# Random-feature attention into a token and channel mixer: q and k transposed by the DMA engines instead of TensorE

## The chip, the cores and the metric

The kernel runs on one core of one Trainium2 chip. The metric is device time in microseconds (us) of one execution. The core has five engines that each work through their own instruction list in order: TensorE (PE, with its weight loads listed as PEld), VectorE (DVE), ScalarE (ACT), GpSimd (POOL) and SyncE (SP). Sixteen DMA engines move data; a transfer is issued from an engine's list, here from POOL (the queue `software_dynamic`, which can change the type on the way), or from SP and ACT (`hardware_dynamic`).

## What is computed

Batch 8, 8 heads, 576 tokens, head width 64, 128 random features; the mixer has a token width of 256 and a channel width of 1536.

```
def phi(x):                       # for q and k, both scaled by 64 ** -0.25
    h = einsum('bhsd,md->bhsm', x, omega) - sum(x * x) / 2
    return exp(h - max(h)) / sqrt(m)
kv  = einsum('bhsm,bhsd->bhmd', k_p, v);   z = sum_s(k_p)
num = einsum('bhsm,bhmd->bhsd', q_p, kv);  den = einsum('bhsm,bhm->bhs', q_p, z)
x = heads side by side of num / (den + 1e-6)            # [8, 576, 512]
u  = x + (relu(x^T @ w_tok1) @ w_tok2)^T                # mixes tokens
out = u + relu(u @ w_ch1) @ w_ch2                       # mixes channels
```

## The kernel before

Everything is computed in fp16 with fp32 sums. Tokens 0 to 511 of a batch are its main part (four per partition), tokens 512 to 575 its tail. Heads are handled in pairs (`hp`, four pairs a batch).

*Loads.* POOL issues all loads and casts fp32 to fp16 on the way: `load_qk` (L76), `load_qk_tail` (L90, L91), `load_v` (L83), `load_v_tail` (L96), and the weights `load_wtok` (L143 to L149), `load_wc1` (L160), `load_wc2` (L163).

*Attention.* The projection needs q and k with the head width on the partitions. `t_main` (L180) transposes eight 128 x 128 blocks (two heads' tokens by two) on TensorE into a PSUM tile `t_ps`, and DVE copies it to `qT` or `kT` (L182); four calls serve a batch. `t_tail` does the same for the tails of q and k (L189, L193). `q_proj` (L247) and `k_proj` (L258) multiply with `bd`, omega twice on a diagonal, and ACT takes the exponential (L197) into `q_p` and `k_p`; `q_tail` (L203) and `k_tail` (L218, four matmuls a batch) do the tail. `k_max` finds each token's largest feature on DVE (L270, L274), its reciprocal (L278), and POOL scales v by it (L279, `v_sc`); `k_tail_max` does that for the tail (L226 to L234). `kv` sums over tokens on TensorE, one head at a time (L290, tail L297), ACT copies the result (L301, `kv_sb`), `num` multiplies by `q_p` (L311, L315), and DVE and ACT divide (L317, L318, L325) into `xm` and `xt`.

*Mixer.* `tok1` (L338, L341), `tok2` (L354), `tok2_tail` (L365), a transpose of u (`tokT`, L377, L378), `ch1` (L392, ReLU on ACT L399) and `ch2` (L404, sum on DVE L413), then the store of `o_sb` by SP (L415; tails L419, L420). `o_sb` has four buffers.

*Order.* No scheduler decides: `at(place, fn, ...)` notes each piece with a place, and the pieces are written out sorted by it, which fixes the order of every engine's list. One step of the place is one head pair; batch b's attention has steps 4b to 4b+4, its token mixing 4(b+1)+0.85 to 4(b+1)+3.85, its channel mixing 4(b+2) to 4(b+3). So the first `ch1` comes at step 8, attention ends near step 33, and the last channel pass, over all tails, fills steps 40 to 44. Batch b is loaded from place 4(b-2)+2.0 on.

Of the kernel before, what the change touches and what calls it, by code (L numbers as in the profile page):

```python
# [9 lines left out]
FP32 = mybir.dt.float32  # L10
# [7 lines left out]
def kernel(  # L18
# [17 lines left out]
    nc = tc.nc  # L36
# [20 lines left out]
    opool = ctx.enter_context(tc.tile_pool(name="outp", bufs=4))  # L57
    pspool = ctx.enter_context(tc.tile_pool(name="ps", bufs=1, space=bass.MemoryType.PSUM))
# [9 lines left out]
    nat = {}  # L68

    def load_qk(b, heads, which):  # L70
        h0, h1 = heads
        src = q if which == "q" else k
        key = (which, b)
        if key not in nat:
            nat[key] = ldpool.tile([P, H, NJ * D], FP16, name=f"{which}_nat", tag=f"{which}_nat")
        nc.gpsimd.dma_start(  # L76
            out=nat[key][:, h0:h1, :],
            in_=src[b, h0:h1, 0:SM, :].rearrange("h (p j) d -> p h (j d)", j=NJ),
        )

    def load_v(b):
        nat["v", b] = ldpool.tile([P, H, NJ * D], FP16, name="v_nat", tag="v_nat")
        nc.gpsimd.dma_start(  # L83
            out=nat["v", b], in_=v[b, :, 0:SM, :].rearrange("h (p j) d -> p h (j d)", j=NJ)
        )

    def load_qk_tail(b):
        t = ldpool.tile([P, H, D], FP16, name="qk_tail", tag="qk_tail")
        nat["qkt", b] = t
        nc.gpsimd.dma_start(out=t[0:ST], in_=q[b, :, SM:S, :].rearrange("h p d -> p h d"))  # L90
        nc.gpsimd.dma_start(out=t[ST:P], in_=k[b, :, SM:S, :].rearrange("h p d -> p h d"))  # L91

    def load_v_tail(b):
        t = ldpool.tile([P, H, D], FP16, name="v_tail", tag="v_tail")
        nat["vt", b] = t
        nc.gpsimd.dma_start(out=t[ST:P], in_=v[b, :, SM:S, :].rearrange("h p d -> p h d"))  # L96

    omega_nat = wpool.tile([P, 2 * D], FP16, name="omega_nat")
    nc.gpsimd.dma_start(out=omega_nat[:, 0:D], in_=omega)
    nc.gpsimd.dma_start(out=omega_nat[:, D : 2 * D], in_=omega)  # L100
    load_qk(0, (0, 2), "q")
    load_qk(0, (0, 2), "k")
    ident16 = wpool.tile([P, P], FP16, name="ident16")
    make_identity(nc, ident16)
    load_qk(0, (2, 4), "q")
    load_qk(0, (2, 4), "k")
    load_qk_tail(0)
    load_v(0)
    load_v_tail(0)
    load_qk(0, (4, 8), "q")  # L110
    load_qk(0, (4, 8), "k")
# [5 lines left out]
    nc.vector.memset(w1t, 0.0)  # L117
# [3 lines left out]
    nc.vector.memset(w2t, 0.0)  # L121
# [6 lines left out]
    vsc_t = [wpool.tile([P, H, 72], FP16, name=f"vsc_t{i}") for i in range(2)]  # L128
    for t in xt:
        nc.vector.memset(t, 0.0)  # L130
    for t in q_pt:
        nc.vector.memset(t[:, 0:ST], 0.0)
        nc.vector.memset(t[:, SM + ST : SM + 2 * ST], 0.0)
    for t in vsc_t:
        nc.vector.memset(t[0:ST], 0.0)
# [5 lines left out]

    def load_wtok():
        nc.gpsimd.dma_start(  # L143
            out=w1m.rearrange("p j t -> p (j t)"),
            in_=moe_w_tok1[0:SM, :].rearrange("(p j) t -> p (j t)", j=NJ),
        )
        nc.gpsimd.dma_start(out=w1t[0:ST, 0, :], in_=moe_w_tok1[SM:S, :])
        nc.gpsimd.dma_start(out=w1t[ST:P, 1, :], in_=moe_w_tok1[SM:S, :])
        nc.gpsimd.dma_start(out=w2raw, in_=moe_w_tok2.rearrange("(i p) s -> p i s", p=P))  # L149
# [9 lines left out]
    def load_wc1():  # L159
        nc.gpsimd.dma_start(out=wc1, in_=moe_w_ch1.rearrange("(i p) c -> p i c", p=P))  # L160

    def load_wc2():
        nc.gpsimd.dma_start(out=wc2, in_=moe_w_ch2.rearrange("(i p) d -> p i d", p=P))  # L163
# [7 lines left out]
    live = {}  # L171


    def t_main(b, half, which):

        src = nat[which, b]
        ps = att_ps([P, 8, P], FP16, "t_ps")
        for i in range(8):
            h, pr = half * 4 + i // 2, i % 2
            nc.tensor.transpose(ps[:, i, :], src[:, h, pr * P : (pr + 1) * P], ident16)  # L180
        sb = apool.tile([P, 8, P], FP16, name=f"{which}T", tag=f"{which}T")
        nc.vector.tensor_copy(out=sb, in_=ps)  # L182
        live[which + "T", b, half] = sb

    def t_tail(b):
        src = nat["qkt", b]
        ps = att_ps([P, NU, P], FP16, "tt_ps")
        for hp in range(NU):
            nc.tensor.transpose(  # L189
                ps[:, hp, :], src[:, 2 * hp : 2 * hp + 2, :].rearrange("p h d -> p (h d)"), ident16  # L190
            )
        sb = apool.tile([P, NU, P], FP16, name="tailT", tag="tailT")
        nc.vector.tensor_copy(out=sb, in_=ps)  # L193
        live["tailT", b] = sb
# [4 lines left out]
    def q_tail(b):  # L199
        sb = live["tailT", b]  # L200
        ps = att_ps([P, SM], FP32, "qt_ps")
        for w in range(2):
            nc.tensor.matmul(  # L203
                ps[:, w * 256 : (w + 1) * 256],
                bd[:, w * M : (w + 1) * M],
                sb[:, :, 0:ST],
                start=True,
                stop=True,
            )
        exp(q_pt[b % 2][:, ST : ST + SM], ps)  # L210

    def k_tail(b, g):
        sb = live["tailT", b]
        if g == 0:
            live["kpt", b] = apool.tile([P, H, M], FP16, name="k_pt", tag="k_pt")
        ps = att_ps([P, 4, M], FP32, "kt_ps")
        for i in range(2):
            nc.tensor.matmul(  # L218
                ps[:, 2 * i : 2 * i + 2, :], sb[:, 2 * g + i, :], bd, start=True, stop=True
            )  # L220
        exp(live["kpt", b][:, 4 * g : 4 * g + 4, :], ps)

    def k_tail_max(b):
        kp = live["kpt", b]
        tmp = apool.tile([P, H, M // 2], FP16, name="mxt", tag="mxt")
        nc.vector.tensor_tensor(  # L226
            out=tmp[ST:P], in0=kp[ST:P, :, 0 : M // 2], in1=kp[ST:P, :, M // 2 : M], op=ALU.max
        )
        mx = apool.tile([P, H], FP16, name="kmt", tag="kmt")
        nc.vector.reduce_max(out=mx[ST:P], in_=tmp[ST:P], axis=AX.X)  # L230
        vs = vsc_t[b % 2]
        with nc.allow_low_precision(reason="fp16 operand of the matmul"):
            nc.vector.reciprocal(out=vs[ST:P, :, D], in_=mx[ST:P])
        nc.gpsimd.tensor_tensor(  # L234
            out=vs[ST:P, :, 0:D],
            in0=nat["vt", b][ST:P],
            in1=vs[ST:P, :, D : D + 1].broadcast_to((ST, H, D)),
            op=ALU.mult,
        )

    def q_proj(b, hp, w):
        sb = live["qT", b, hp // 2]
        if w == 0:
            live["qp", b, hp] = apool.tile([P, 2, 4, P], FP16, name="q_p", tag="q_p", bufs=3)
        ps = att_ps([P, 4, P], FP32, "q_ps")
        i0 = (hp % 2) * 4
        nc.tensor.matmul(  # L247
            ps, bd[:, w * M : (w + 1) * M], sb[:, i0 : i0 + 4, :], start=True, stop=True
        )
        exp(live["qp", b, hp][:, w], ps)  # L250

    def k_proj(b, hp, i):
        sb = live["kT", b, hp // 2]
# [3 lines left out]
        for pr in range(2):  # L257
            nc.tensor.matmul(  # L258
                ps[:, 2 * pr : 2 * pr + 2, :],
                sb[:, (hp % 2) * 4 + 2 * i + pr, :],  # L260
                bd,
                start=True,
                stop=True,
            )
        exp(live["kp", b, hp][:, i], ps)

    def k_max(b, hp):
# [9 lines left out]
        with nc.allow_low_precision(reason="fp16 operand of the matmul"):  # L277
            nc.vector.reciprocal(out=vs[:, :, D], in_=mx)  # L278
        nc.gpsimd.tensor_tensor(  # L279
            out=vs[:, :, 0:D],  # L280
            in0=nat["v", b][:, 2 * hp : 2 * hp + 2, :].rearrange("p h (j d) -> p (h j) d", d=D),
# [4 lines left out]
    def kv(b, hp, i):  # L286
        h = 2 * hp + i
        ps = att_ps([P, D + 1], FP32, "kv_ps")
        for j in range(NJ):
            nc.tensor.matmul(  # L290
                ps,
                live["kp", b, hp][:, i, j, :],
                live["vsc", b, hp][:, i * 4 + j, 0 : D + 1],
                start=(j == 0),
                stop=False,
            )
        nc.tensor.matmul(  # L297
            ps, live["kpt", b][:, h, :], vsc_t[b % 2][:, h, 0 : D + 1], start=False, stop=True
        )
        sb = apool.tile([P, D + 1], FP16, name="kv_sb", tag="kv_sb", bufs=4)  # L300
        nc.scalar.copy(out=sb, in_=ps)  # L301
        live["kv", b, h] = sb

    def num(b, hp, i):
# [3 lines left out]
        sb = live["kv", b, h]  # L308
        ps = att_ps([P, NJ + 1, D + 1], FP32, "num_ps")
        for j in range(NJ):  # L310
            nc.tensor.matmul(  # L311
                ps[:, j, :], live["qp", b, hp][:, j % 2, 2 * i + j // 2, :], sb, start=True, stop=True
            )
        c0 = ST + (h % 2) * 256 + hp * ST - (b % 2) * ST
# [107 lines left out]

    def load_batch(b):
        load_qk(b, (0, H), "q")
        load_qk(b, (0, H), "k")
        load_qk_tail(b)
# [3 lines left out]
    at(0.02, load_wtok)  # L430
    at(0.30, load_batch, 1)
    at(0.60, load_wc1)
    at(0.90, load_wc2)
    at(1.2, permute_w2)
    for b in range(2, B):
# [78 lines left out]
```

The softmax here doesn't subtract the row's maximum and nothing guards it: scores larger than these inputs give would overflow.

## Time and profile before

| what | value |
|---|---|
| median of 3 runs | 348.16 us (347.2 to 349.61) |
| profiled execution, its own time | 348.58 us |
| its span, first to last instruction | 346.8 us |
| TensorE busy in the span | 310.2 us (89%) |
| DVE, ACT, POOL busy | 176.3, 173.5, 89.0 us |
| DMA issues from POOL, q and k of one batch | 512 KB each, 6.2 and 8.2 us to landing (medians) |
| stores from SP, 256 KB | 2.3 us to landing (median) |

The page cuts the span into 40 equal slices and gives each engine's busy share in tenths, the clock granted to TensorE in tenths, and the DMA engines' share and rate. Below it stand the chain of waits that ended last, groups of instructions by line, and DMA issues. A size in KB of a DMA issue is that of its fp16 destination where it casts. Matmuls are pipelined: the start of one to the start of the next tells what it costs, its own duration does not.

### The profile page before, as it was taken

The page shows a single profiled execution, that of the slowest core. Times are in us where ns is not written, and L with a number is a line of the kernel's source. Part 1 is how long each engine was busy: PE and PEld are TensorE (multiplying, and loading weights), DVE is VectorE, ACT ScalarE, POOL GpSimd, SP SyncE. Part 2 cuts the span into 40 slices and gives each one's busy share as a digit, 9 for nine tenths or more (in the row PEclk, how much of TensorE's full clock was granted, in tenths as well). Part 3 has the DMA queues.
Part 4 walks back from the last instruction along what each step waited for, and adds up shares of the span by engine and source line. Part 5 has one row for each costly group of instructions (what it writes and reads, how often), then busy time and mean ns, then how long its engine had stood idle before and what let it go on. Part 6 is the DMA issues. An engine that isn't in the chain of part 4 may idle for free.

```text
span 346.8 us, 5958 instructions
## 1 busy us (share of the span) xinstructions
PE 310.2 (89%) x2337; PEld 170.4 (49%) x2337; DVE 176.3 (51%) x423; ACT 173.5 (50%) x397; POOL 89.0 (26%) x106
## 2 busy tenths in 40 slices
PE   1537666999999999999999999999999899999994
PEld 1324344555655565556555655565555444444441
DVE  2546679546764575557654755576546414302011
ACT  1426663973397338743774378436753450160620
POOL 8687264243114411350225012011211100000000
PEclk9958999999999999999999999999999999999999
DMA  6999999309400950096009800011001001102013
GB/s 71 160 193 208 206 194 191 41 7 188 104 30 3 176 121 30 2 154 143 32 1 135 163 32 0 32 47 46 1 32 60 33 0 60 62 0 91 32 30 92
DMA packets 45916, 27.78 MB, mean 80 GB/s; under 512 B 14144, under 2 KB 40640, under 8 KB 45888
## 3 DMA queue, kind: packets, MB, share of 16 engines
q0 software_dynamic: 40640, 17.96, 41.3%
q1 hardware_dynamic: 5248, 9.44, 7.7%
q8 instruction: 18, 0.29, 0.3%
q14 instruction: 10, 0.08, 0.1%
HBM read 35.91 MB, written 9.44 MB: 131 GB/s over the span
## 4 chain that ended last, share of the span: by engine, by line
PE 77%; DVE 9%; ACT 4%; POOL 4%; DMA 3%; issue 2%; DVEq 0%; ACTq 0%; POOLq 0%
PE h_ps L392 27%; PE h_ps L404 25%; PE h_ps L338 3%; PE k_ps L258 3%; PE ht_ps L354 3%; PE q_ps L247 3%; PE t_ps L180 3%; DMA w1m<-in_moe_w_tok_dram 3%; PE num_ps L311 2%; DVE xm L318 2%; PE kv_ps L290 2%; DVE km L274 2%; ACT k_p L197 1%; ACT q_p L197 1%; PE uT_ps L377 1%
## 5 line engine op out<-in xcount | busy, mean ns | idle before, releaser
L404 PE MATMUL h_ps<-wc,r 128*128 128x512 f16 x432 | 98.1, 379 | 0.5 <-DVE ut L372 0.4
L392 PE MATMUL h_ps<-uT,wc 128*128 128x512 f16 x384 | 94.2, 379 | 3.7 <-DVE uT L378 3.7
L399 ACT ACTIVATE r<-h_ps 128x512 f16<-128x512 f32 x108 | 64.3, 601 | 46.2 <-PE h_ps L392 45.3
L279 POOL TENSOR_TENSOR v_sc<-v_nat,v_sc 128x512 f16<-128x512 f16 x32 | 34.1, 1065 | 164.5 <-DVE rc L317 81.5
L404 PEld LDWEIGHTS <-r 128*128 128x128 f16 x432 | 41.2, 98 | 46.2 <-issue 1.2
L392 PEld LDWEIGHTS <-wc 128*128 128x128 f16 x432 | 40.1, 98 | 42.6 <-issue 4.7
L325 ACT ACTIVATE xt<-num_ps,rc 64x64 f16<-64x64 f32 x64 | 19.7, 309 | 63.4 <-DVE xm L318 33.8
L197 ACT ACTIVATE k_p<-k_ps 128x512 f16<-128x512 f32 x64 | 37.7, 603 | 23.9 <-PE k_ps L258 23.9
L413 DVE TENSOR_TENSOR o_sb<-um,h_ps 128x512 f32<-128x512 f16 x32 | 21.9, 686 | 54.3 <-PE h_ps L404 54.3
L270 DVE TENSOR_TENSOR mx<-k_p 128x512 f16<-128x512 f16 x32 | 13.5, 422 | 51.9 <-ACT k_p L197 51.9
L197 ACT ACTIVATE q_p<-q_ps 128x512 f16<-128x512 f32 x64 | 36.4, 594 | 5.8 <-PE q_ps L247 5.2
L318 DVE TENSOR_TENSOR xm<-num_ps,rc 128x256 f16<-128x256 f32 x64 | 27.2, 425 | 2.4 <-DVE rc L317 0.2
L258 PE MATMUL k_ps<-bd,kT 128*128 128x256 f16 x128 | 24.9, 284 | 2.2 <-ACT xt L325 2.2
L357 DVE TENSOR_TENSOR um<-xm,ht_ps 128x512 f16<-128x512 f16 x32 | 21.8, 683 | 8.0 <-PE ht_ps L354 7.6
L247 PE MATMUL q_ps<-qT,bd 128*128 128x512 f16 x64 | 23.7, 395 | 0.0
L274 DVE TENSOR_REDUCE km<-mx 128x8 f16<-128x512 f16 x32 | 22.0, 686 | 1.1
L258 PEld LDWEIGHTS <-kT 128*128 128x128 f16 x128 | 12.7, 101 | 17.0 <-issue 4.0
L311 PEld LDWEIGHTS <-q_p 128*128 128x128 f16 x256 | 15.3, 98 | 10.9 <-issue 4.2
L290 PE MATMUL kv_ps<-v_sc,k_p 128*128 128x65 f16 x256 | 15.1, 195 | 5.0 <-POOL v_sc L279 4.7
L290 PEld LDWEIGHTS <-k_p 128*128 128x128 f16 x256 | 13.7, 99 | 12.1 <-issue 8.0
L311 PE MATMUL num_ps<-kv_sb,q_p 128*128 128x65 f16 x256 | 17.3, 194 | 2.2 <-ACT kv_sb L301 1.9
L354 PE MATMUL ht_ps<-r,w2m 128*128 128x512 f16 x64 | 19.0, 379 | 0.1
(80 smaller groups left out, 350.1 us busy)
## 6 DMA issues: line engine op xcount, KB each, us to landing
out_dram<-o_sb SPq DMA_DIRECT2D x32, 256.0 KB, 2.3
v_nat<-in_v_dram POOLq DMA_DIRECT2D x8, 512.0 KB, 10.3
q_nat<-in_q_dram POOLq DMA_DIRECT2D x7, 512.0 KB, 6.2
k_nat<-in_k_dram POOLq DMA_DIRECT2D x7, 512.0 KB, 8.2
wc<-in_moe_w_ch_dram POOLq DMA_DIRECT2D x2, 1536.0 KB, 18.2
out_dram<-o_sb SPq DMA_DIRECT2D x8, 128.0 KB, 2.3
qk_tail<-in_q_dram POOLq DMA_DIRECT2D x8, 64.0 KB, 7.7
qk_tail<-in_k_dram POOLq DMA_DIRECT2D x8, 64.0 KB, 7.4
```

Of the source, the lines that this page charges most:

```text
L197: nc.scalar.activation(out=out, in_=in_, func=AF.Exp, bias=0.0, scale=c_scale)
L247: nc.tensor.matmul(ps, bd[:, w * M : (w + 1) * M], sb[:, i0 : i0 + 4, :], start=True, stop=True)
L258: nc.tensor.matmul(ps[:, 2 * pr : 2 * pr + 2, :], sb[:, (hp % 2) * 4 + 2 * i + pr, :], bd, start=True, stop=True,)
L274: nc.vector.reduce_max(out=mx, in_=tmp, axis=AX.X)
L279: nc.gpsimd.tensor_tensor(out=vs[:, :, 0:D], in0=nat["v", b][:, 2 * hp : 2 * hp + 2, :].rearrange("p h (j d) -> p (h j) d", d=D), in1=vs[: ...
L290: nc.tensor.matmul(ps, live["kp", b, hp][:, i, j, :], live["vsc", b, hp][:, i * 4 + j, 0 : D + 1], start=(j == 0), stop=False,)
L311: nc.tensor.matmul(ps[:, j, :], live["qp", b, hp][:, j % 2, 2 * i + j // 2, :], sb, start=True, stop=True)
L318: nc.vector.tensor_tensor(out=live["x", b][:, :, h * D : (h + 1) * D], in0=ps[:, 0:NJ, 0:D], in1=rc[:, 0:NJ].unsqueeze(2).broadcast_to((P, ...
L354: nc.tensor.matmul(ps, w2m[:, tb, j, :], live["r1", b][:, tb, :], start=(tb == 0), stop=(tb == NT - 1))
L392: nc.tensor.matmul(ps, wc1[:, db, cb * P : (cb + 1) * P], uT[:, db].rearrange("p j c -> p (j c)"), start=(db == 0), stop=(db == ND - 1),)
L399: nc.scalar.activation(out=live["r3", c][:, cb, :], in_=ps, func=AF.Relu)
L404: nc.tensor.matmul(ps, live["r3", c][:, cb, j * P : (j + 1) * P], wc2[:, cb, :], start=(cb == 0), stop=(cb == NCB - 1),)
```

## The change

For batches 1 to 7, q and k take another way. POOL issues one DMA each that casts a batch's whole q or k into a scratch tensor in DRAM, [8 heads x 288, 128] in fp16, where one row is two neighbouring tokens (parity, d). SP then issues one DMA transpose of it into `qT` or `kT`, [128, 8 x 288] in SBUF: rows are (token parity, d), columns token pairs. Tails are the last 32 columns of each head. Batch 0 is still transposed by TensorE, two heads at a time, into the same layout; heads 0 and 1 and the tails come in fp32 by hardware queues (SP and ACT) and are cast on DVE.

v is loaded in fp32 by SP with two tokens (512 bytes) a row, and scaled into fp16 on POOL; for batch 0 the scaling is done by DVE. The tail of k now has four heads' tails on one 128-row tile: `k_tail` is two matmuls and one exponential a batch, the scaled v tail `vz` is zero outside its head, and `kv` makes both heads of a pair into one PSUM tile with two tail matmuls of 130 columns and one copy. Eight matmuls on zeros (`warm`) run at the start. w_tok, the casts of batch 1, and both channel weights (in halves) are issued before the first step; clears of constant tiles move later. Batch b's transposes and v loads stand at 4(b-2)+2.8 (batch 1: 0.9), its casts at 4(b-2)+2.0.

The diff, cut to its core:

```diff
+    def cast_dram(b, which):
+        src = q if which == "q" else k
+        t = dpool.tile([H * SP2, 2 * D], FP16, name=f"{which}16", tag=f"{which}16")
         nc.gpsimd.dma_start(
-            out=nat[key][:, h0:h1, :],
-            in_=src[b, h0:h1, 0:SM, :].rearrange("h (p j) d -> p h (j d)", j=NJ),
-        )
+            out=t.rearrange("(a x) y -> a (x y)", a=P),
+            in_=src[b].rearrange("h (e s) d -> (h e) (s d)", e=P // H),
+        )
+    def load_T(b, which):
+        t = ldpool.tile([P, H, SP2], FP16, name=f"{which}T", tag=f"{which}T", bufs=2)
+        nc.sync.dma_start_transpose(
+            out=t.rearrange("p h c -> p (h c)"), in_=live[which + "16", b]
+        )
     def load_v(b):
-        nat["v", b] = ldpool.tile([P, H, NJ * D], FP16, name="v_nat", tag="v_nat")
+        t = ldpool.tile([P, H, NJ, D], FP32, name="v_nat", tag="v_nat", bufs=2)
+        for e in range(2):
+            nc.sync.dma_start(
+                out=t[:, :, 2 * e : 2 * e + 2, :].rearrange("p h w d -> p h (w d)"),
+                in_=v[b, :, e * NP2 : (e + 1) * NP2, :].rearrange("h (p w) d -> p h (w d)", w=2),
+            )
...
+    stage_qk(nc.sync, 0, 2, "q")
+    stage_qk(nc.scalar, 0, 2, "k")
...
+    for i in range(8):
+        nc.tensor.matmul(warm_ps, warm[:, 0:P], warm, start=True, stop=True)
...
-    def k_tail(b, g):
+    def k_tail(b):
+        kt = apool.tile([P, H, ST // 2], FP16, name="k_tt", tag="k_tt")
+        nc.vector.tensor_copy(out=kt, in_=sb[:, :, NP2:SP2])
...
+        for hh in range(4):
+            r = slice(32 * hh, 32 * hh + 32)
+                nc.vector.reciprocal(out=vs[r, hh, :, D], in_=mx[r])
+            eng.tensor_tensor(
+                out=vs[r, hh, :, 0:D],
...
-    def kv(b, hp, i):
+    def kv(b, hp):
...
+        for w in range(2):
             nc.tensor.matmul(
                 ps,
+                live["kpt", b][:, 2 * g + w, :],
+                vz[b % 2][:, h0 : h0 + 2, 2 * g + w, 0 : D + 1],
...
+    def load_first():
+        load_wtok()
+        for which in "qk":
+            cast_dram(1, which)
+        load_wc1(0)
+        load_wc1(1)
+        load_wc2(0)
+        load_wc2(1)
...
+    at(-0.90, load_first)
...
+    for h0 in range(0, H, 2):
+        at(h0 / 2 - 0.92, t_main, h0, "q")
+        at(h0 / 2 - 0.85, t_main, h0, "k")
+    def load_batch_2(b):
+        for which in "qk":
+            load_T(b, which)
+        load_v(b)
+        load_v_tail(b)
-    for b in range(2, B):
-        at(4 * (b - 2) + 2.0, load_batch, b)
+    for b in range(1, B):
+        if b > 1:
+            at(4 * (b - 2) + 2.0, load_batch, b)
+        at(4 * (b - 2) + 2.8 if b > 1 else 0.9, load_batch_2, b)
...
-            at(u + 0.55, k_max, b, hp)
-            at(u + 1.32, kv, b, hp, 0)
-            at(u + 1.40, kv, b, hp, 1)
-            at(u + 1.58, num, b, hp, 0)
-            at(u + 1.66, num, b, hp, 1)
+            at(u + 0.55, k_max, b, hp, nc.gpsimd if b else nc.vector)
+            at(u + 1.30, kv, b, hp)
+            at(u + 1.72, num, b, hp, 0)
+            at(u + 1.82, num, b, hp, 1)
```

## The prediction, made before the changed kernel was run

> **What bounds the kernel now.** I read the busy slices of the page first, then three stretches of the windows view cut where the first `ch1` matmul starts (60.87 us) and where the last attention work is gone (271.67 us), then who TensorE waited for in the first stretch, then TensorE's timeline, the chain of waits there, and the DMA rows.
>
> ```profile
> PE   1537666999999999999999999999999899999994
> ...
> PEclk9958999999999999999999999999999999999999
> DMA  6999999309400950096009800011001001102013
> GB/s 71 160 193 208 206 194 191 41 7 188 104 30 3 176 121 30 2 154 143 32 1 135 163 32 0 32 47 46 1 32 60 33 0 60 62 0 91 32 30 92
> ```
> One slice is 8.67 us. For seven slices TensorE is part busy and the DMA engines are full, near 200 GB/s; from slice eight it is the reverse.
>
> ```profile
> 0.00:60.87 60.87, 32.74 (x331) 21.17 (x332) 36.75 (x99) 27.11 (x68) 38.46 (x52) 0.92 1.30 175
> 60.87:271.67 210.80, 208.02 (x1658) 117.20 (x1658) 124.54 (x297) 123.42 (x289) 50.49 (x54) 1.00 0.39 65
> 271.67:346.80 75.13, 69.43 (x350) 32.01 (x349) 15.03 (x27) 22.92 (x41) 0.00 (x0) 0.99 0.15 46
> ```
> The columns are the stretch, its length, and busy time of PE, PEld, DVE, ACT and POOL, then clock, DMA share and rate. The middle stretch is TensorE's alone (208.0 of 210.8 us), so each TensorE microsecond taken out there shortens the span. The last stretch has no attention work; nothing in it changes. The first is bound by something else, and has to be worked out apart.
>
> ```profile
> PE t_ps L180 <- DMA q_nat<-in_q_dram: 5.1, 3, 2.5
> PE kv_ps L290 <- POOL v_sc L279: 4.7, 2, 4.0
> PE om_ps L138 <- POOL ident masks.py:199: 4.6, 1, 4.6
> ```
> Those are TensorE's longest waits before 60.87 us (total, times, longest): the first loads, then POOL, which scales v between its own DMA issues.
>
> ```profile
> 121.48 0.61 PE L180 MATMUL t_ps<-ident,q_nat 128*128 128x128 f16 x8
> 121.92 0.38 PE L247 MATMUL q_ps<-qT,bd 128*128 128x512 f16 x1
> ...
> 125.84 0.29 PE L290 MATMUL kv_ps<-v_sc,k_p 128*128 128x65 f16 x4
> 125.96 0.19 PE L297 MATMUL kv_ps<-vsc_t,k_pt 128*128 128x65 f16 x1
> ```
> ```profile
> 134.23 0.38 PE L218 MATMUL kt_ps<-bd,tailT 128*128 128x256 f16 x2
> 134.45 1.03 PE L392 MATMUL h_ps<-uT,wc 128*128 128x512 f16 x4
> ```
> Durations overlap, so a matmul's cost is read from start to start: eight transposes 121.92 - 121.48 = 0.44 us, 0.055 us each; four 65-column matmuls 0.12 us, 0.030 each; two 256-column ones 0.22 us, 0.11 each.
>
> ```profile
> q0 software_dynamic: 40640, 17.96, 41.3%
> q1 hardware_dynamic: 5248, 9.44, 7.7%
> ```
> Per packet: 41.3% of 16 x 346.8 us over 40640 = 56 ns for about 1 KB read and 0.44 KB written; 7.7% over 5248 = 81 ns for 1.8 KB stored.
>
> **The change, part by part.**
>
> *Middle stretch, transposes.* 176 `t_ps` transposes lie in it (the windows view of that tile), and 20 of `tt_ps` (five batches): 196 x 0.055 = 10.8 us out. `k_tail` goes from four 256-column matmuls to two in six batches: 12 x 0.11 = 1.3 us out. The tail matmul of `kv` becomes 130 columns wide, at about the 0.055 of the 128-column transposes: 8 per batch in 6.25 batches, 50 x 0.025 = 1.25 us in. Net -10.9 us, all on the path, as TensorE idles 2.8 us in that stretch.
>
> The Trainium skill, "TensorE: Matmul & The Clock Gate", Part 4, puts a 128 x 128 transpose at about 275 ns in a kernel's context; by that figure, as an estimate, the 196 would be worth 53.9 us. The trace's 0.055 us start to start decides, since neighbours fill the rest.
>
> *What is off that path.* DVE loses 22 evictions of 0.69 us and gains per batch a 256-column copy and three more reciprocals (0.21 us each); ACT loses one exponential (0.67) and half of its `kv_sb` copies (0.24 each). They are 59% busy there: nothing. POOL scales v from fp32: 1.06 us a piece, at worst doubled for twice the bytes; its tail scaling of 1.05 us becomes four pieces of half the columns, some 0.55 us each. It drops six DMA issues of 0.7 to 0.95 us per batch for two. It is 24% busy there, so this is covered by idle POOL time; what it costs if not is a rival below.
>
> *SP's queue.* It gains two transposes and six v loads per batch, some 0.55 us an issue as for its stores. `load_batch_2(b)` stands at step 4(b-2)+2.8; its first transpose waits for the cast and for the last `q_proj` and `k_proj` of batch b-2 (+3.04 to +3.26), its v load for the last `v_sc` (+3.55). Behind it stand the stores of `o_sb` placed at +3.25 and +3.75. They go out up to half a step (4 us) late, while four `o_sb` buffers and a next use at +6.25 give three steps (26 us): nothing.
>
> *Price of a DMA transpose, T.* No row shows one. It brings 0.59 MB. From below: the stores' row, 328 packets of 1.8 KB x 81 ns / 16 engines = 1.7 us. From above: each of its 2304 source rows of 256 B a packet at the 56 ns of the casting queue, 2304 x 56 / 16 = 8.1 us. I take 2.5 us, half as much again as the stores, which use the same kind of queue without a cast and differ by the short rows; both ends are kept.
>
> The Trainium skill, "DMA: Bandwidth & Descriptors", Latency and other measured facts, gives 261 GB/s for a DMA transpose; by that T would be 2.3 us, an estimate that no run shown here supports yet, and the arrival below 1 us earlier. Its Specifications hold that line rate needs at least 512 B a transfer, which speaks against the change's 256-byte rows.
>
> *Price of a v load, V.* fp16 at 200 GB/s: 0.59 MB, 2.95 us. Now 2304 packets of 512 B; at the packet rate of the full slices (200 GB/s of 442 B on 16 engines, 35 ns) 5.1 us. I take 4.2.
>
> *First stretch, compute.* The first exponential of `q_p` starts at 12.41 us. Now q and k of heads 0-1 come by hardware queues (2.3 us from issue to landing for a store of that size) and are cast on DVE (0.42 to 0.69 us each), transposed, evicted and projected: about 7.3 us, 5.1 us sooner. The eight warm-up matmuls, at most 0.43 us each, lie beside those loads and end before omega is there. From there eight steps follow, each one turn of this loop:
>
> ```profile
> 44.82 0.49 ACT k_p L197
> ...
> 45.33 0.44 DVE mx L270
> ...
> 45.79 0.70 DVE km L274
> ...
> 46.58 0.21 DVE v_sc L278
> ```
> The turn is 5.6 us (`q_p` starts at 37.84, 42.90, 48.95, 54.60) and keeps its order. 8 x 5.6 = 45 us; the wait of 4.0 us on POOL's `v_sc` goes, as batch 0 scales v on DVE. That puts 0.69 us a step and some 2.5 us of tail work onto DVE, partly in its gaps, partly paid for by the evictions it loses in batch 1; I add 0.7 us. Compute alone reaches `ch1` at 53 us.
>
> *First stretch, DMA.* `q_tail` and `k_proj` of batch 2 stand just around the first `ch1`, and their data is the last of a long list. At 200 GB/s of fp16: q and k of batches 0, 1, 2 at 5.9 us each (a cast into DRAM counted like one into SBUF: it reads the same bytes), w_tok 3.0, both channel weights, which stand ahead of batch 2, 15.7; then V for batches 0 and 1 and four T. With 2 us of start: 2 + 17.7 + 3.0 + 15.7 + 2V + 4T = 38.4 + 8.4 + 10 = 56.8 us. That is later than 53, so the transfers decide (POOL issues them early, since it no longer scales batch 0's v between them): the middle stretch starts at 56.8 in place of 60.87, -4.1 us.
>
> *Sum.* 346.8 - 10.9 - 4.1 = 331.8 us of span, and the 1.8 us by which the profiled execution's 348.58 stands above its span: 333.6. The median of the runs is 0.4 below that execution, so 333.
>
> **Rivals.**
> (B) The transfers hide. For: T and V at their lower ends give 38.4 + 5.9 + 6.8 = 51.1 us, below the 53 of compute. Against: the DMA row is already full. Then 346.8 - 10.9 - 7.9 + 1.8 - 0.4 = 329; with the 3.7 us that TensorE waits for `uT` also gone, 326.
> (C) Slower: a slow transpose. Place: `qT` and `kT` of batch 2, on which TensorE, in order, holds up all of `ch1`. For: short rows, four transposes in a stretch of full DMA. The start of the middle stretch may slip to 60.87 + 10.9 = 71.8 before the gain is used up: T = (71.8 - 46.8) / 4 = 6.3 us. At 8.1 the arrival is 79.2 and the time 346.8 - 10.9 + 18.3 + 1.4 = 356. Later batches have 35 us each, so only this one pays.
> (D) POOL becomes the wait: `kv` of a batch's first pair needs `v_sc` and four tail pieces, 1.06 + 4 x 0.55 = 3.3 us, after 2.5 us of DVE work, inside some 0.9 of a step (7.5 us). At doubled prices it is 6.6 + 2.5, some 1.6 us over, times 7 batches = 11 us: 344 to 346. Against: POOL's low load.
>
> **How the numbers follow.** Forecast 0.50, B 0.25, C 0.15, D 0.10. The likeliest case alone spans 329 to 339 (T from 1.7 to 4). The range takes in B's lower end, a little more for a shorter turn (324), and C up to T near 7 (352). About 1% is what a measurement of this kernel can tell. Faster: the forecast, B and a third of D, 0.78; same: the rest of D, 0.07; slower: 0.15.
>
> **What would show it.** The 12-matmul groups of `ch2` should lie closer together, each batch's turn in the middle at 33.5 us against 35.4. A DMA transpose from issue to landing near 2.5 us alone, more among other traffic, proves or breaks the price; the first `ch1` matmul between 53 and 59 us the start. If TensorE's longest wait is for `qT` or `kT`, C is right in kind; if it is POOL's `v_sc` or the tail's, D is; if the middle stretch is not nearly full, the forecast is wrong in its main term.

## The result, and the profile after

The changed kernel is slower: 356.56 us (356.16 to 358.29, four runs) against 347.72 us (347.2 to 349.61), a ratio of 1.0254 (95% interval 1.0201 to 1.0306). Its profiled execution took 356.16 us and has a span of 354.4 us. Of all the runs below, one (366.65 us, of eight of e1_gate) fell into a slower state and is left out of the medians and ratios.

The three stretches tell where that came from. Below are windows of after: its head in three parts, cut where the first `qT` transpose is issued (21.0 us), where it has landed (52.4 us) and where the first `ch1` matmul starts (76.75 us); then the middle and the last channel pass. The columns are those of the windows shown for before.

```profile
0.00:21.00 21.00, 8.24 (x37) 3.83 (x37) 8.42 (x22) 4.65 (x7) 11.37 (x22) 0.82 1.10 213
21.00:52.40 31.40, 11.25 (x103) 7.74 (x103) 17.46 (x52) 8.13 (x20) 0.00 (x0) 0.55 1.18 169
52.40:76.75 24.35, 17.31 (x150) 10.16 (x151) 15.67 (x45) 12.72 (x31) 7.63 (x10) 0.82 1.07 223
76.75:279.35 202.60, 198.13 (x1450) 106.47 (x1450) 111.41 (x295) 113.00 (x259) 43.83 (x56) 1.00 0.49 111
279.35:354.40 75.05, 69.49 (x350) 32.07 (x349) 15.47 (x29) 23.16 (x41) 0.00 (x0) 1.00 0.14 46
```

The middle is 202.60 us in place of 210.80 (-8.2), the last pass 75.05 in place of 75.13 (-0.1), the head 76.75 in place of 60.87 (+15.9). Together that is the 7.6 us by which the span grew. So the change gave what it was built on, TensorE time in the middle, and lost twice as much before it.

The busy slices of after (8.86 us each) show the head as a hole in TensorE's row at slice six (44 to 53 us), with the DMA row full.

```profile
PE   6326307869999999999999999999999999999994
...
PEclk9755656899999999999999999999999999999999
DMA  8999999996558267907770897011001100201113
```

In the head of after, two waits of TensorE stand far above the rest (total, times, longest):

```profile
PE qt_ps L261 <- DMA qT<-q: 10.5, 1, 10.5
PE tt_ps L251 <- DVE k_natt L248: 9.7, 1, 9.7
```

**The first wait** is for batch 1's transpose. The chain of waits of after holds it, and TensorE's timeline shows its end:

```profile
7.87 13.13 DMA q<-in_q_dram
21.02 31.34 DMA qT<-q
```
```profile
52.41 0.61 PE L261 MATMUL qt_ps<-qT,bd 128*128 128x256 f16 x2 [10.46 <-DMA qT<-q]
```

The cast of q into DRAM took 13.13 us, and then the transpose 31.34 us from issue to landing. Now SP's queue in after (start, length of the issue itself, instruction):

```profile
21.02 11.36 SPq L85 DMA_TRANSPOSE qT<-q  x1
32.48 19.84 SPq L85 DMA_TRANSPOSE kT<-k  x1
52.38 1.20 SPq L94 DMA_DIRECT2D v_nat<-in_v_dram  x2
53.62 2.86 SPq L103 DMA_DIRECT2D v_tail<-in_v_dram  x4
56.66 2.54 SPq L85 DMA_TRANSPOSE qT<-q  x1
59.36 2.54 SPq L85 DMA_TRANSPOSE kT<-k  x1
```

Batch 1's pair holds SP for 31 us, and batch 1's v loads queue behind it until 52.38. Batch 2's pair, the same instructions on the same sizes, takes 2.54 us each. Over all seven batches the medians from issue to landing are 6.4 and 5.0 us:

```profile
qT<-q SPq DMA_TRANSPOSE x7, 6.4
kT<-k SPq DMA_TRANSPOSE x7, 5.0
```

What is different for batch 1 is in POOL's list:

```profile
12.36 0.78 POOL L212 DMA_DIRECT2D wc<-in_moe_w_ch_dram  x1 [2.44 <-DMA q_nat<-in_q_dram]
14.78 0.76 POOL L212 DMA_DIRECT2D wc<-in_moe_w_ch_dram  x1 [1.64 <-DMA k_nat<-in_k_dram]
16.48 0.82 POOL L218 DMA_DIRECT2D wc<-in_moe_w_ch_dram  x1 [0.95 <-DMA w1m<-in_moe_w_tok_dram]
18.16 0.82 POOL L218 DMA_DIRECT2D wc<-in_moe_w_ch_dram  x1 [0.86 <-DMA w2raw<-in_moe_w_tok_dram]
18.98 0.52 POOL L77 DMA_DIRECT2D q<-in_q_dram  x1
19.50 0.51 POOL L77 DMA_DIRECT2D k<-in_k_dram  x1
```

Just before the transpose, POOL issues both channel weights (3.1 MB) and batch 2's casts (1.2 MB). The last weight half lands 30.6 us after its issue, at 48.8 us, the casts at 49.5 and 52.5; `qT` lands at 52.36. The transpose is in another queue, SP's, yet it ended when they ended. The DMA rows of after tell how the two queues shared the engines (packets, MB, share of 16 engines), first from 26 to 42 us, then from 43 to 48 us, when it was mostly the casts that were left:

```profile
q0 software_dynamic: 2012, 2.31, 90.8%
q1 hardware_dynamic: 2012, 0.52, 33.7%
...
q0 software_dynamic: 94, 0.91, 97.7%
q1 hardware_dynamic: 92, 0.02, 5.6%
```

Packet for packet the two queues went on alike: 126 each per us in the first window, 18 each per us in the second. But POOL's packets average 1.1 KB and then 9.7 KB, while a transpose moves one row of 256 bytes a packet (0.52 MB in 2012). So it was not held until POOL's loads were done, as in one line by order of issue: it moved beside them all the time, with less than a fifth of the bytes moved, and then a fortieth.

**The second wait** lies in batch 0. DVE's timeline of after:

```profile
12.72 0.21 DVE L341 RECIPROCAL v_sc<-km 128x8 f16<-128x8 f16 x1
19.54 0.69 DVE L342 TENSOR_TENSOR v_sc<-v_nat,v_sc 128x512 f16<-128x512 f32 x1 [6.61 <-DMA v_nat<-in_v_dram]
...
21.72 0.66 DVE L248 CAST k_natt<-stt_k 32x1024 f16<-32x1024 f32 x1
```

DVE now scales batch 0's v, and waits 6.61 us for it to land. Behind that wait stand the clears, an eviction and the cast of the tail (`k_natt`, 21.72), which TensorE waits for before it can go on with its tail transposes. The `q_p` exponentials of the first, second and third pair start at 8.90, 11.39 and 33.68 us: 24.8 us for two steps, where two turns of 5.6 were expected.

### The profile page after: what moved, and what is told of

The parts are those of the page before. It is cut to its first block, busy times and chain, and to the rows that moved or that the text cites. A ratio compares the mean times of both kernels' runs of the same rounds, so it can differ in the third digit from the quotient of the medians.

```text
span 354.4 us, 5567 instructions
## 1 busy us (share of the span) xinstructions
PE 304.4 (86%) x2089; PEld 160.3 (45%) x2089; DVE 168.4 (48%) x440; ACT 161.7 (46%) x357; POOL 62.8 (18%) x88
## 4 chain that ended last, share of the span: by engine, by line
PE 61%; DMA 14%; DVE 10%; ACT 10%; issue 3%; POOL 0%; SPq 0%; DVEq 0%; ACTq 0%
PE h_ps L470 27%; PE h_ps L458 17%; DMA qT<-q 9%; DMA q<-in_q_dram 4%; PE ht_ps L420 3%; ACT k_p L255 3%; ACT q_p L255 3%; PE h_ps L404 3%; ACT r L465 3%; PE q_ps L310 2%; PE k_ps L321 2%; DVE km L337 2%; PE num_ps L377 2%; DVE xm L384 1%; DVE vz L297 1%
## 5 line engine op out<-in xcount | busy, mean ns | idle before, releaser
L465 ACT ACTIVATE r<-h_ps 128x512 f16<-128x512 f32 x108 | 65.1, 613 | 36.0 <-PE h_ps L458 35.7
L342 POOL TENSOR_TENSOR v_sc<-v_nat,v_sc 128x512 f16<-128x512 f32 x28 | 29.6, 1058 | 205.5 <-DVE v_sc L341 111.6
L377 PEld LDWEIGHTS <-q_p 128*128 128x128 f16 x256 | 16.7, 103 | 16.0 <-issue 7.0
L377 PE MATMUL num_ps<-kv_sb,q_p 128*128 128x65 f16 x256 | 18.7, 201 | 4.8 <-ACT kv_sb L367 4.5
L337 DVE TENSOR_REDUCE km<-mx 128x8 f16<-128x512 f16 x32 | 21.9, 686 | 1.1
L383 DVE RECIPROCAL rc<-num_ps 128x5 f32<-128x5 f32 x64 | 11.7, 182 | 13.9 <-PE num_ps L381 13.4
L404 PE MATMUL h_ps<-xm,w1m 128*128 128x512 f16 x64 | 16.9, 388 | 0.9 <-ACT r L465 0.9
```

The lines of the kernel that those rows point to most:

```text
L337: nc.vector.reduce_max(out=mx, in_=tmp, axis=AX.X)
L342: eng.tensor_tensor(out=vs[:, :, 0:D], in0=live["v", b][:, 2 * hp : 2 * hp + 2].rearrange("p h j d -> p (h j) d"), in1=vs[:, :, D : D + 1] ...
L377: nc.tensor.matmul(ps[:, j, :], live["qp", b, hp][:, j % 2, i, j // 2, :], sb, start=True, stop=True)
L404: nc.tensor.matmul(ps, w1m[:, j, tb * P : (tb + 1) * P], live["x", b][:, j, :], start=(j == 0), stop=False)
L465: nc.scalar.activation(out=live["r3", c][:, cb, :], in_=ps, func=AF.Relu)
```

## The experiments

The theories were these (their letters are not those of the prediction's rivals). (A) The first transposes move 256 bytes a packet and share the DMA engines, packet by packet, with POOL's queue of large packets, so they get a small part of the rate until that queue is empty. (B) The first transposes are slow by themselves, whatever runs beside them. (C) Only the sum of bytes counts: all that is listed has to come in by then. (D) What is left of the delay is batch 0's chain on DVE (the wait for v, then the tail). (E) It is TensorE's clock, granted at 0.50 to 0.76 from 9 to 53 us of after, where before had 1.00 from 35 us on. The first four kernels ran together, beside runs of before with a median of 348.73 us; the last three together, beside 348.14 us.

**e1_gate** holds the channel weights and batch 2's casts on POOL until batch 1's `kT` is there (`gate` multiplies a few of its columns into a tile that nothing reads). Nothing else in the order changes.

```diff
...
+    def gate(ap):
+        nc.gpsimd.tensor_tensor(out=gate_t, in0=ap, in1=ap, op=ALU.mult)
     def load_first():
         load_wtok()
         for which in "qk":
             cast_dram(1, which)
+
+    def load_rest():
+        gate(live["kT", 1][:, H - 1, SP2 - D : SP2])
         load_wc1(0)
...
+    at(0.91, load_rest)
```

> The changed kernel with one thing added: POOL reads the last columns of batch 1's kT before it issues the channel weights and the casts of batch 2, so that batch 1's transposes run without them. Theory A (the transposes were starved: their 256-byte packets take turns with POOL's packets of 1.5 to 18 KB, so they end only when POOL's queue is empty): qT of batch 1 lands within 5 to 9 us of its issue instead of 31.3, the 10.5 us wait of TensorE for it goes, the first ch1 matmul moves from 76.75 to 60 to 66 us, the time is 340 to 347 us. Theory B (the first transposes are slow in themselves, because they are first or because they read what was just written): qT still takes over 20 us, and the weights are then late as well, time 356 us or more. Theory C (only the sum of bytes counts, as the prediction had it): qT lands sooner, but batch 2's data, now behind the weights, lands as late as before or later and TensorE waits at step 8 instead, time 350 to 358 us.

Measured: 344.31 us (median of seven), ratio 0.9893 (0.9857 to 0.9929). SP's queue of e1_gate:

```profile
20.95 2.97 SPq L85 DMA_TRANSPOSE qT<-q  x1
24.03 3.51 SPq L85 DMA_TRANSPOSE kT<-k  x1
```

Issued at the same moment as in after, `qT` lands 6.6 us later in place of 31.3 and `kT` 6.4 us in place of 21.9. The first `ch1` starts at 64.82 us, 11.9 earlier. The same bytes move in the head in the end, and the first transposes are hardly slower than later ones (medians 6.1 and 5.4): B falls, and so does C as the reason for the 31 us. A small wait for batch 2's `qT` (2.8 us) is new; that one took 11.7 us: batch 2's casts now stand behind the weights and were late, and batch 3's (51.43 and 51.98 us) run beside it.

**e2_small** leaves the order and cuts the weight loads into pieces of 128 columns, so that their packets are a fraction of the size.

```diff
     def load_wc1(part):
-        c0, c1 = part * DC // 2, (part + 1) * DC // 2
-        nc.gpsimd.dma_start(
-            out=wc1[:, :, c0:c1], in_=moe_w_ch1[:, c0:c1].rearrange("(i p) c -> p i c", p=P)
-        )
+        for c0 in range(part * DC // 2, (part + 1) * DC // 2, P):
+            nc.gpsimd.dma_start(
+                out=wc1[:, :, c0 : c0 + P],
+                in_=moe_w_ch1[:, c0 : c0 + P].rearrange("(i p) c -> p i c", p=P),
+            )
```

(`load_wc2` likewise, by 128 output columns.)

> The changed kernel with the channel weights read in rows of 512 bytes (16 DMAs instead of 4), all else as it is. Theory A (turns are taken packet by packet, so the size of the other queue's packets sets how long the transposes wait): the 288 packets per DMA engine of batch 1's two transposes now stand against turns that are three to six times shorter, and qT lands 10 to 18 us after its issue instead of 31.3, while the weights land later; TensorE's wait for qT shrinks to 0 to 3 us and the time to 346 to 352 us. Theory B (transposes slow in themselves) and C (only the sum counts): more packets for the same bytes, qT lands no sooner than 31 us after its issue, time 356 us or more.

Measured: 350.65 us, ratio 1.0064 (1.0029 to 1.01); `qT` of batch 1 lands after 12.0 us, `kT` after 14.2, and the first `ch1` starts at 69.07. SP's queue of e2_small:

```profile
20.63 5.93 SPq L85 DMA_TRANSPOSE qT<-q  x1
26.67 7.95 SPq L85 DMA_TRANSPOSE kT<-k  x1
```

With the same bytes issued in the same order, the transpose is 2.6 times as fast. TensorE's wait for it is 4.1 us, a little over the 3 that A allowed. It isn't a pure test: POOL needs 20 issues in place of 4 and is paced by them (its last weight piece goes out at 41.36 us, not 18.16), so batch 2's casts come after the transposes. But POOL's queue was not empty beside them. Its DMA rows from 26 to 30 us:

```profile
q0 software_dynamic: 1343, 0.33, 81.8%
q1 hardware_dynamic: 1375, 0.35, 65.1%
```

Again the packets are nearly equal in number, but POOL's now average 0.25 KB, and SP's go through at 344 per us in place of 126. So the size of the other queue's packets sets the share, as A says, and C falls. How much of the 31.3 us is due to the weights and how much to the casts stays open; as an estimate, at 126 per us the 2304 packets of `qT` take 18 us.

**e3_beside** turns it round: four extra loads of 768 KB of weights into DRAM tiles that nothing reads (`spare`) are issued behind batch 4's casts, so that a later pair of transposes meets what batch 1's met.

```diff
...
     def load_batch(b):
         for which in "qk":
             cast_dram(b, which)
+        if b == 4:
+            for i, t in enumerate(spare):
+                c0 = (i % 2) * DC // 2
+                nc.gpsimd.dma_start(out=t, in_=moe_w_ch1[:, c0 : c0 + DC // 2])
```

> The changed kernel with four useless loads added behind the casts of batch 4 on POOL's queue, 6.3 MB of channel weights cast into DRAM in 3 KB rows, where the trace is quiet; batch 4's transposes, 5.6 and 4.5 us from issue to landing, then run beside them. Theory A (starved by the packets of the other queue): qT and kT of batch 4 take 12 to 25 us to land, those of batches 3, 5, 6 and 7 still 4.5 to 7; the time hardly moves, as they have over 30 us. Theory B (only first transposes are slow): batch 4's stay at 4.5 to 7 us.

One run, 358.12 us. The four loads, issued from 95.5 to 97.3 us, take up to 26.0 us. Batch 4's `qT` takes 20.4 us to land and its `kT` 9.8 (12 to 25 were expected of both); batch 3's take 5.8 and 5.0, batch 5's 7.0 and 5.3. SP's queue of e3_beside, batches 3, 4 and 5:

```profile
72.50 2.92 SPq L85 DMA_TRANSPOSE qT<-q  x1
75.59 2.88 SPq L85 DMA_TRANSPOSE kT<-k  x1
104.76 13.96 SPq L85 DMA_TRANSPOSE qT<-q  x1
118.81 6.24 SPq L85 DMA_TRANSPOSE kT<-k  x1
138.19 3.62 SPq L85 DMA_TRANSPOSE qT<-q  x1
141.91 3.29 SPq L85 DMA_TRANSPOSE kT<-k  x1
```

From 112 to 118 us its DMA rows have as many packets on both queues:

```profile
q0 software_dynamic: 692, 1.03, 94.0%
q1 hardware_dynamic: 692, 0.18, 22.1%
```

A transpose in the middle of the kernel becomes slow as soon as such loads are beside it. With e1_gate and the packet counts, this shows A from both sides. TensorE doesn't wait for it there, as batch 4's data has over 30 us to arrive.

**e4_order** makes the whole order one of need: batch 1's casts wait until batch 0's v has landed, w_tok follows them, the first channel weight and batch 2's casts wait for batch 1's v, the second for batch 2's v, and batch 3 is loaded from step 8.0 on.

```diff
     def load_first():
-        load_wtok()
+        gate(live["v", 0][:, H - 1, NJ - 1, :])
         for which in "qk":
             cast_dram(1, which)
+        load_wtok()
+    def load_rest():
+        gate(live["v", 1][:, H - 1, NJ - 1, :])
         load_wc1(0)
         load_wc1(1)
+    def load_last():
+        gate(live["v", 2][:, H - 1, NJ - 1, :])
         load_wc2(0)
         load_wc2(1)
...
+    at(0.91, load_rest)
+    at(7.6, load_last)
```

> The changed kernel with POOL's loads put in order of need by three small POOL reads that wait: casts of batch 1 after batch 0's v has landed, then w_tok; first channel weight and casts of batch 2 after batch 1's v; second channel weight after batch 2's v; casts and transposes of batch 3 two steps later. Theory A: DVE's 6.6 us wait for batch 0's v and TensorE's 10.5 us wait for qT both go, steps of 5.6 us run through, first ch1 at 53 to 58 us, time 332 to 340 us. Theory C (sum of bytes): the list up to batch 2's kT is 10 to 15 us shorter by the second channel weight, but the gates leave DMA gaps; first ch1 at 58 to 66 us, time 338 to 346 us. Theory B: no better than 354 us.

Measured: 343.09 us, ratio 0.9847 (0.9824 to 0.9871); first `ch1` at 62.72 us. Both lie in the ranges expected under C (58 to 66 and 338 to 346) and above those under A (53 to 58 and 332 to 340), so these numbers alone would speak for C. The waits say otherwise: none for `qT` is left, and DVE's wait for v is 1.4 us in place of 6.6. The longest wait of TensorE in the head of e4_order is the tail of batch 0:

```profile
PE tt_ps L251 <- DVE k_natt L248: 5.3, 1, 5.3
```

So no transfer of q and k holds TensorE up any more, and a chain inside batch 0 remains, which A's range had left out and D names: the `q_p` of the first three pairs start at 8.70, 11.37 and 28.74 us.

**e5_tail** starts from e4_order and moves batch 0's tail: its transposes and casts before the first step, `q_tail` to 0.50, `k_tail` and `k_tail_max` to where the later batches have them, one clear earlier.

```diff
-    at(0.95, clear)
+    at(0.06, clear)
...
-    at(1.105, t_tail, "k")
-    at(1.106, t_tail, "q")
+    at(-0.81, t_tail, "k")
+    at(-0.80, t_tail, "q")
...
-        at(g - 0.20 if b else 1.15, q_tail, b)
-        at(g + 0.42 if b else 1.12, k_tail, b)
...
+        at(g - 0.20 if b else 0.50, q_tail, b)
+        at(g + 0.42, k_tail, b)
...
```

> The ordered kernel (e4_order) with batch 0's tails of q and k cast, transposed and projected ahead of its first k_max, and the clears of constant tiles moved up, so that they no longer stand on DVE behind the wait for v. Theory D (the head is lost to one chain: from the first q_p at 8.7 us to that of the third pair at 28.7 us it takes 20 us where two steps of 5.6 take 11.2, because DVE works off v, clears, tails and four reciprocals one after the other with TensorE waiting): the third pair starts at 21 to 25 us, first ch1 at 55 to 59 us, time 335 to 339. Rival: the first steps wait for the loads of heads 2 to 7 or for batch 1's transposes instead, first ch1 over 61 us, time 341 or more.

Measured: 339.24 us (338.47 to 339.72), ratio 0.974 (0.9714 to 0.9765), first `ch1` at 59.10 us. The wait for `k_natt` is 1.6 us. The `q_p` exponentials on ACT, one line a pair from the second pair on:

```profile
16.75 1.33 ACT L255 ACTIVATE q_p<-q_ps 128x512 f16<-128x512 f32 x2
25.31 1.06 ACT L255 ACTIVATE q_p<-q_ps 128x512 f16<-128x512 f32 x2
30.91 1.06 ACT L255 ACTIVATE q_p<-q_ps 128x512 f16<-128x512 f32 x2
36.63 1.06 ACT L255 ACTIVATE q_p<-q_ps 128x512 f16<-128x512 f32 x2
43.08 1.06 ACT L255 ACTIVATE q_p<-q_ps 128x512 f16<-128x512 f32 x2
```

D holds: the third pair starts 3.4 us earlier (25.31 against 28.74), and the steps from there are 5.6 to 6.5 us, as in e4_order. All three numbers end just above the ranges expected under D (21 to 25, 55 to 59, 335 to 339): the first pair now starts 3.1 us later, at 11.81, with the tail ahead of it. This version beats both kernels.

**e6_warm** adds to e5_tail ten matmuls on zeros in each of the first eight steps, to raise TensorE's clock.

```diff
+    def keep_warm(n):
+        ps = mix_ps([P, SM], FP32, "keep_ps")
+        for _ in range(n):
+            nc.tensor.matmul(ps, warm[:, 0:P], warm, start=True, stop=True)
+    for u in range(8):
+        at(u + 0.285, keep_warm, 4)
+        at(u + 0.90, keep_warm, 6)
```

> e5_tail with ten 512-column matmuls on zeros in each of steps 0 to 7 (four after k_proj, six after num), where TensorE waits; their results are not used. Theory E (without its transposes TensorE is too idle in the head to get its full clock; the granted clock is 0.50 to 0.75 from 9 to 53 us in e4_order and was 1.00 from 35 us before): clock 0.9 to 1.0 from some 15 us on, steps of 5.2 us in place of 5.7, first ch1 3 to 5 us sooner than e5_tail, time 3 to 5 us shorter. Rival (the step is ACT's and DVE's loop and the clock does not matter): within 1 us of e5_tail, or up to 4 us longer, as the zeros stand ahead of kv and the next q_proj.

Measured: 339.84 us, ratio 0.976 (0.9736 to 0.9785). The windows of the first 40 us, e5_tail and then e6_warm:

```profile
0.00:40.00 40.00, 25.18 (x177) 15.19 (x178) 27.57 (x80) 16.03 (x35) 9.90 (x22) 0.80 0.91 175
```
```profile
0.00:40.00 40.00, 29.23 (x223) 16.13 (x224) 27.58 (x80) 16.03 (x35) 10.43 (x22) 1.00 0.94 179
```

The clock goes from 0.80 to 1.00, and nothing is gained: the third to sixth pairs start at 25.32, 30.93, 36.64 and 43.08 us, within 0.02 of e5_tail, and the first `ch1` at 60.36 in place of 59.10, later and not 3 to 5 us sooner. E falls. With TensorE faster and the turn unchanged, the turn is not TensorE's. The chain of waits of e5_tail has the loop that sets it: from 24.58 to 30.91 us it runs over ACT (`q_p`, `k_p`, `xt`) and DVE (`mx` to `xm`) alone, but for issue times of 0.1 us and less.

**e7_before_warm** puts the same matmuls into the kernel before, to see whether it would gain by them.

```diff
+    warm = wpool.tile([P, 4 * P], FP16, name="warm")
+    nc.vector.memset(warm, 0.0)
+    def keep_warm(n):
+        ps = mix_ps([P, SM], FP32, "keep_ps")
+        for _ in range(n):
+            nc.tensor.matmul(ps, warm[:, 0:P], warm, start=True, stop=True)
+    for u in range(8):
+        at(u + 0.285, keep_warm, 4)
+        at(u + 0.90, keep_warm, 6)
```

> The kernel before with the same ten matmuls on zeros in each of steps 0 to 7. Theory E: its clock is already 1.00 from 35 us, and 0.54 to 0.87 only from 17 to 35 us, so at most 1 to 2 us are gained; more likely within 1 us of the kernel before, 346 to 350 us. Rival (clock does not matter): the same or up to 4 us longer.

Measured: 353.41 us, ratio 1.0137 (1.0106 to 1.0168); its first `ch1` starts at 65.66 us in place of 60.87. That is 5.3 us over before, more than either expectation allowed, though its clock in the first 60.87 us is 0.94 against 0.92 for before. No support for E here either. And the gain of e5_tail over before isn't a matter of clock: up to its first `ch1` its clock is 0.86, lower than before's.

## Why the prediction was wrong

- **The step that failed is "First stretch, DMA".** It put all transfers into one list at one rate, each done in order of need, with batch 2's `qT` and `kT` last at 56.8 us, and four transposes at 2.5 us each. The trace has no such list: while both queues had work, each moved as many packets as the other (2012 and 2012 from 26 to 42 us), whatever their size. So the transposes of batch 1, issued from 21 us on, got through only as POOL's queue drained, and that queue had been filled with weights not needed before the first `ch1`, forecast at 56.8 us, and with batch 2's casts. e1_gate shows it by changing only that: 31.3 us become 6.6. The same price in e3_beside (20.4 us) shows that it belongs to what runs beside the transpose, not to batch 1.
- **A rival of the prediction had the size but neither the place nor the cause.** Its (C) forecast a slower kernel at 356 us through waits for transposes, with T = 8.1 us for each and batch 2 as the place. Measured were 31.3 and 21.9 us to landing for batch 1's pair, medians of 6.4 and 5.0 over all seven, and a first `ch1` at 76.75 us against C's 79.2. "Later batches have 35 us each, so only this one pays" held, but for the first pair, which the working skipped. It also took SP's waiting to be free in general; in the head it kept batch 1's v loads until 52.38 us.
- **T was near as a spacing, not as a landing.** Undisturbed, SP spends 2.4 to 4.0 us on a transpose and starts the next then: 2.5 was at the lower edge. But the prediction's own sign was issue to landing near 2.5 us, and the shortest landing of after is 4.5.
- **"First stretch, compute" was also too short.** Forecast were a first `q_p` at 7.3 us, eight steps in 45.7 us, and `ch1` at 53. After's first `q_p` starts at 8.90. The error is in "0.69 us a step and some 2.5 us of tail work onto DVE, partly in its gaps": the scaling waited 6.6 us for v, which the working let arrive in time, and from the cast of `k_natt` (21.72 us) to the last `vz` (29.34 us) the tail holds the order of DVE's list for 7.6 us. In e5_tail, with both mended, eight steps run from 11.81 to 60.10 us: 48.3 us, 2.6 more than forecast, after a start 4.5 us later than forecast.
- **The two parts of the loss.** Forecast 56.8 us for the first `ch1`, measured 76.75: 20 us. The order of transfers alone (e4_order, 62.72) takes off 14.0, batch 0's tail (e5_tail, 59.10) another 3.6, and 2.3 remain.
- **The middle was right in kind, and a quarter short.** Forecast -10.9 us, measured -8.2. TensorE's busy time fell by 9.9 (208.02 to 198.13), so the count of removed transposes holds up to 1 us. Idle time rose from 2.8 to 4.5 us, as TensorE now outruns ACT's ReLU after `ch1`. The waits there, after:

```profile
PE h_ps L458 <- DVE uT L444: 2.7, 4, 1.4
PE h_ps L458 <- ACT r L465: 1.3, 3, 0.4
PE h_ps L404 <- ACT r L465: 0.9, 3, 0.4
```

  The two on `r` (2.2 us) aren't in that stretch of before. ACT was "off that path" by its share of busy time, but not at every point.
- **POOL.** The prediction's rival (D) did not come: scaling v from fp32 costs 1.06 us a piece as before, four tail pieces 2.7 us, and none of TensorE's long waits is on them.
- **What the change is worth.** With its transfers and batch 0's tail in order (e5_tail), 2.6% under before. The forecast of 333 us lies 6 below that: 2.7 us from the middle and 2.3 from its start make up most of it.

Two places of the Trainium skill bear on the failed step. "DMA: Bandwidth & Descriptors", Queues, rings and completion order, says that each DMA engine goes round the queue rows that have work, a whole packet at a time. The equal counts agree with it, if the profile's packets are the page's: 2012 each in after, 692 each in e3_beside, 1343 and 1375 in e2_small. The rule could have told that a queue of short packets gets a share by packets and not by bytes. The 261 GB/s that the same page gives for a DMA transpose with a non-contiguous middle dimension (Latency and other measured facts) is, as an estimate, 2.3 us for 0.59 MB, against 2.4 to 4.0 us between issues here, and says nothing on 31.3 us beside a full queue. The prediction used it without that condition, and the page has a higher figure for the contiguous case.

## What to carry to other kernels

Where transfers of two queues overlap, don't add their bytes up at one rate: ask of each needed transfer what the other queues hold at its issue, and how large those packets are. Hold bulk loads that are needed late until the short-row transfers that are needed soon have landed; here one small POOL instruction that reads the awaited tile did it, worth 11.9 us at the start of the middle. And when an engine takes over work in a filling phase, check what it will wait for there and what its list holds behind that wait.

## What the runs showed of the hardware

- While both had work, POOL's queue and SP's moved as many packets as each other, whatever their size: 2012 each (1.1 KB and 256 bytes) from 26 to 42 us of after, 692 each (1.5 KB and 256 bytes) from 112 to 118 us of e3_beside, 1343 and 1375 (0.25 KB and 256 bytes) from 26 to 30 us of e2_small.
- A DMA transpose of 0.59 MB took 6.6 us to land, or 31.3 us, issued at the same time in the same program but for 4.3 MB in another queue. The issue instruction itself is held as well (2.97 against 11.36 us, and 19.84 for the next), so everything behind it on the issuing engine is late too.
- A granted clock of 0.80 instead of 1.00 over 40 us cost nothing (e5_tail and e6_warm start their third to sixth pairs within 0.02 us of each other, up to 43.08), where ACT and DVE set the turn.
- 80 added matmuls on zeros cost the kernel before 1.4%, although TensorE was busy for 32.74 of its first 60.87 us; what they displaced there stays open.
